# A planner's rules and one buffer: a third unit's gate inputs loaded with the first loads, and large loads held back on the queue

## The chip, the cores and the metric

The kernel runs on one core of a Trainium2 chip. The metric is the device time of one execution in microseconds (us), 591.86 as the median of three runs (590.08 to 592.78). The engines are TensorE (PE), VectorE (DVE), ScalarE (ACT), GpSimd (POOL, hardly used) and SyncE (SP), whose queue issues all DMA transfers of this kernel.

## The reference

Two stages follow each other. The first is a gated linear recurrence over time with a complex gate, for 4 batches, 8 heads, 768 steps and a head dimension of 48:

```
mag = sqrt(a_re^2 + a_im^2);  scale = min(mag, 0.999) / (mag + 1e-6)
ar, ai = a_re*scale, a_im*scale                 # per step and row d
S_re, S_im = ar*S_re - ai*S_im + k v^T,  ar*S_im + ai*S_re
y[t] = q[t] @ S_re
```

The second takes the 3072 rows of y (8 heads x 48 = 384 columns) through two matrix products with an activation between them: `h = x @ w_in` (384 x 2048), `g = 0` for h <= -1, `h` for h >= 1 and `(h+1)^2/4` between, `out = g @ w_out` (2048 x 384).

## The kernel before, in words

Time is cut into units of 256 steps: 12 units, three per batch. Two units make a block of 512 columns; there are six blocks. Three kinds of work run at once.

*Gates of a unit* (`gates(u)`). The decay and the phase of the recurrence are turned into running sums. `ai_u` holds a_re and a_im (one load of 768 KB). ACT and DVE alternate: Relu, Ln, Exp on ACT, products and clamps on DVE (L544, L547), Square and Ln on ACT, L556 and L565 on DVE; then three running sums of the decay on DVE (L575), two Exp on ACT, and the product of k and q with the decays (L594, tile `kq_u`). Then Arctan on ACT, three running sums of the phase (L604), the fraction of a turn (L620, L626), sine and cosine on ACT, and two turns on DVE: L681 makes x = kq times cosine, then kq = kq times sine. Each result is *spread* by five DMAs over the tiles `hd`, where each head has its rows together: 48, 48, 32 and twice 16 partitions. A unit thus has ten spreads, five from x and five from kq.

*Attention of a unit* (`attend(u)`). In chunks of 128 steps PE makes scores (`sc`, L834, which need all of a head's spreads), DVE masks them (`am`, L842), PE transposes keys (`tp`), ACT copies them (`kT`), PE makes state products (`dp`, L807) and DVE adds them to the state (`st`, L817, L819); PE makes the values (`yp`, L873, L881), and ACT copies them into `xr` and `ys`. After a block's last chunk six small DMAs (the hand-over, `xr<-ys`) put the rows of the split heads into their places. Then ACT and DVE split xr into a high and a low part (`xH` L967, `xL` L974).

*MoE of a block* (`moe(blk)`). For each of 16 groups of 128 hidden columns PE makes h (nine matmuls of 128x512, L997), ACT makes s from it (L1022 and, in the first block, L1032 and L1036), DVE makes g (L1041), ACT its high part (`gh`, L1055), DVE its low part (`gl`, L1059), and PE, three groups later, adds nine matmuls into the output (L1072).

*Weights* (`weights`). Sixteen pieces i0, i1, o0, i2, o1, i3, ... of 768 KB arrive as 64-bit numbers. DVE makes a float of each by two or three shifts (L401 into the one buffer `y`, L410, L419); ACT rounds it to its high part (L425). The low part is a subtraction on DVE (L430) from the fourth piece on (`LO_PE = 3`); for the first three PE forms it (`rest`, L439 and L440: float minus high part) in two halves through one PSUM bank, and ACT copies each half (L454). The raw pieces lie in buffers that later hold xH and xL: four buffers in turn for the first four pieces (`HOME = 4`), two from then on.

*Order.* All of this is recorded as operations with costs, reads, writes and due times (`Plan.op`), and `Plan.order` makes each engine's order from a list schedule. On each engine the ready operation with the earliest due time goes first. `HOLD` lets DVE and ACT stay idle for a more urgent operation that is about to be ready; SP has no such rule. Each engine's queue then runs in that order, and an operation that waits holds back all behind it. PE's idle stretches ahead of the first MoE matmul are filled with matmuls that nothing reads (L1123).

*Buffers.* Four buffers `g0` to `g3` of 768 KB hold the tiles `ai`, `x` and `kq` of the units in turn; unit 1's x, kq and V are *guests* in the places of weights that arrive late (`guest(("o", 7), ...)`). ai_2 takes g0 after ai_0, so its load waits until unit 0's last turn has read ai_0.

Of the kernel before, what the change touches and what calls it, by code (L numbers as in the profile page):

```python
# [10 lines left out]
F32 = mybir.dt.float32  # L11
# [7 lines left out]
P = 128  # L19
# [7 lines left out]
NJ = DM // P  # L27
NF = DFF // P
CH = 128
U = 256  # L30
# [24 lines left out]
LOAD, MOVE = 410.0, 240.0  # L55
TABLE = 1294
FIRST = 63000
SLACK = 1.0
LAG = 3
SPREADS = 0  # L60
SPREAD = ("SP", "ACT")
HOLD = {'DVE': (2, 0.0), 'ACT': (2, 0.0)}
WINDOW = (0.0, 0.7)
EARLY = (0.15, 0.7)
HEAD = ((15000, 8000), (8000, 2000))
HOME = 4
SPARE = 1
LEAD = 9000
WARM = 0.75
ABS_ACT = 4  # L70
LO_PE = 3
INFLATE = 1.6
SPLIT_DUE = 3000

# [38 lines left out]
class Plan:  # L113
# [43 lines left out]
    def order(self):  # L157
        ops = self.ops
        n = len(ops)
        succ = [[] for _ in range(n)]  # L160
        for i, o in enumerate(ops):
            for p in o[3]:
                succ[p].append(i)
        due = [0.0] * n
        big = 1e12
        for i in range(n - 1, -1, -1):
            eng, cost, _, _, d, dma = ops[i]
            t = big if d is None else d
            if dma:
                own = DMA_FIX + DMA_END + dma + 600  # L170
            else:
                own = cost * (INFLATE if eng in ("ACT", "DVE") else 1.0) + LAT[eng]
            for s in succ[i]:
                t = min(t, due[s] - own)
            due[i] = t
        left = [len(o[3]) for o in ops]
        ready = [0.0] * n
        end = [0.0] * n
        start = [0.0] * n
        free = {e: 0.0 for e in ("PE", "DVE", "ACT", "SP", "POOL")}  # L180
        wait = {e: [] for e in free}
        avail = {e: [] for e in free}
        queue = {}

        def enable(i):
            heapq.heappush(wait[ops[i][0]], (ready[i], i))

        for i in range(n):
            if not left[i]:
                enable(i)  # L190
        done = 0
        taken = set()
        forced = []
        while done < n:
            if forced:
                i = forced.pop()
                e = ops[i][0]
                t = max(free[e], ready[i])
            else:
                best = None  # L200
                for e in free:
                    while avail[e] and avail[e][0][1] in taken:
                        heapq.heappop(avail[e])
                    while wait[e] and wait[e][0][1] in taken:
                        heapq.heappop(wait[e])
                    if avail[e]:
                        t = free[e]
                    elif wait[e]:
                        t = max(free[e], wait[e][0][0])
                    else:  # L210
                        continue
                    if best is None or t < best[0]:
                        best = (t, e)
                t, e = best
                while wait[e] and wait[e][0][0] <= t:
                    _, i = heapq.heappop(wait[e])
                    if i not in taken:
                        heapq.heappush(avail[e], (due[i], i))
                d, i = heapq.heappop(avail[e])
                if e in HOLD:  # L220
                    late = t + ops[i][1]
                    soon = [
                        (r, j)
                        for r, j in wait[e]
                        if j not in taken
                        and r < late
                        and due[j] + HOLD[e][1] < d
                        and late - r > HOLD[e][0] * (r - t)
                    ]
                    if soon:  # L230
                        heapq.heappush(avail[e], (d, i))
                        free[e] = min(soon)[0]
                        continue
            taken.add(i)
            eng, cost, _, _, _, dma = ops[i]
            start[i] = t
            free[e] = t + cost
            if dma:
                q = queue.setdefault(eng, [0.0] * LANES)
                t = max(t, q[-LANES])  # L240
                q.append(max(t + DMA_FIX, q[-1]) + dma)
                end[i] = q[-1] + DMA_END
                start[i] = t
                free[eng] = t + cost
            else:
                end[i] = t + cost
            done += 1
            for s in succ[i]:
                left[s] -= 1
                lat = LAT[eng]  # L250
                if dma or s in self.loose:
                    lat = 0
                elif ops[s][0] == eng:
                    lat = SAME[eng]
                ready[s] = max(ready[s], end[i] + lat)
                if not left[s]:
                    enable(s)
            nxt = self.glued.get(i)
            if nxt is not None and not left[nxt]:
                forced.append(nxt)  # L260
        self.start, self.end, self.due = start, end, due
        return sorted(range(n), key=lambda i: (start[i], i))
# [44 lines left out]
def gated_scan_moe(  # L307
# [57 lines left out]

    V_, A_, PE_ = nc.vector, nc.scalar, nc.tensor

    def dma(nbytes, dst, src, r=(), w=(), due=None, rate=LOAD, eng="SP"):
        queue = {"SP": nc.sync, "ACT": nc.scalar, "POOL": nc.gpsimd}[eng]
        return pl.op(  # L370
            eng,
            DMA_ISSUE,
            lambda: queue.dma_start(dst(), src()),
            r=r,
            w=w,
            dma=nbytes / rate,
            due=due,
        )

    def table(name):  # L380
# [112 lines left out]


    heads, vt = {}, {}

    def gates(u):
        b, part = divmod(u, NPART)
        last = part == NPART - 1
        shape = [P, NJ, 2, U]  # L500
        N = NJ * U
        AI = tl(turn_of("g", 4), [P, 2, NJ, U], F32, f"ai_{u}")
        if u == 1:
            block = lambda t: t.rearrange("p (j e n) -> p j e n", j=NJ, e=2)
            X, KQ = guest(("o", 7), "x_1", block), guest(("o", 6), "kq_1", block)
# [8 lines left out]
        if u == 0:  # L514
            for e in range(2):
                dma(
                    size,
                    lambda e=e: AI.get()[:, e],
                    lambda e=e: ari[u, :, e],
                    w=[(AI, e)],  # L520
                )
        else:
            dma(2 * size, lambda: AI.get(), lambda: ari[u], w=[a, i])

        def ac(out, src, f, r, w, tab=False, **kw):
            acc_ = kw.get("accum_out")
# [63 lines left out]
        ac(X1, X0, AF.Exp, [x0], [x1], True, scale=-1.0)  # L590
        ac(X0, X0, AF.Exp, [], [x0], True)

        dma(2 * size, lambda: KQ.get(), lambda: kq[u], w=[KQ])
        ve(dve(2 * N), lambda: V_.tensor_tensor(KQ.get(), KQ.get(), X.get(), op=ALU.mult), [X], [KQ])  # L594

        yield
# [133 lines left out]
        turn(KQ, 1)  # L730
        for g in range(3):
            spread(g, 1, KQ)

# [402 lines left out]
    attend(0)  # L1138
    list(second)
    attend(1)  # L1140
    for n, (kind, i) in enumerate(todo):
        weights(n, kind, i, ("xH1", "xL1", "xH0", "xL0")[n % 4] if n < HOME else ("xH1", "xL1")[n % 2])
    for blk in range(NBLK):
        for u in BLOCKS[blk]:
            if u > 1:
                list(gates(u))
                attend(u)
        if blk == NBLK - 1:
            for k in range(NF):
# [256 lines left out]
```

## Time and profile before

| what | value |
|---|---|
| median of three runs | 591.86 us (590.08 to 592.78) |
| the profiled execution | 590.78 us, its span (first to last instruction) 589.0 us |
| busy: PE, DVE, ACT | 565.3, 448.0, 388.8 us |
| DVE busy in 0 to 20, 20 to 40, 40 to 60, 60 to 80 us | 11.17, 19.13, 14.97, 19.86 us of 20 |
| PE's granted clock, mean | 0.981 |
| first MoE matmul | 84.13 us |

PE's busy time holds the filling matmuls too, so the first 84 us are read from the waits and not from the share. In the rows, `x<-kq,ai` names what an instruction writes and reads, with buffer numbers left out; `ai<-in_ari_dram` is the load of a unit's gate inputs, `raw_i` and `raw_o` are the loads of weights.

### The profile page before, as it was taken

To read this page: it belongs to the slowest core of one execution; us is meant where nothing else is said; L and a number is where in the kernel's file an instruction comes from. 1 tells how busy PE (TensorE), PEld (TensorE's weight loads), DVE (VectorE), ACT (ScalarE), POOL (GpSimd) and SP (SyncE) were. 2 spreads that over 40 slices of the span, in tenths; PEclk is the share of its full clock that TensorE was granted. 3 is DMA by queue.
4 is the path that set the end of the run, shared out by engine and by line. 5 is a ranking of instruction groups with operands and counts; after the bars stand their busy time and mean duration, and the time that the engine had idled before them with its cause. 6 is when DMAs were issued, how large, how long until landed. Compare 5 with 4: busy or idle time off the path is not lost.

```text
span 589.0 us, 9922 instructions
## 1 busy us (share of the span) xinstructions
PE 565.3 (96%) x3920; PEld 481.1 (82%) x3920; DVE 448.0 (76%) x638; ACT 388.8 (66%) x629; POOL 1.5 (0%) x18
## 2 busy tenths in 40 slices
PE   6987989999999999999999999999999999999995
PEld 6776878888878888888888888888888888888883
DVE  4996999999988988769888788897874544555443
ACT  7756779999788675756765676656643323469962
POOL 1000000000000000000000000000000000000000
PEclk9888989999999999999999999999999999999998
DMA  8577155482561430440700530701511300077821
GB/s 348 187 202 228 47 172 200 143 303 84 160 201 37 115 128 1 117 174 20 218 24 1 168 125 19 230 13 49 154 55 55 80 1 3 19 281 260 281 84 59
DMA packets 21798, 74.26 MB, mean 126 GB/s; under 512 B 3888, under 2 KB 8496, under 8 KB 21744
## 3 DMA queue, kind: packets, MB, share of 16 engines
q1 hardware_dynamic: 21744, 73.55, 38.3%
q8 instruction: 33, 0.54, 0.4%
q14 instruction: 21, 0.17, 0.1%
HBM read 48.76 MB, written 4.72 MB: 91 GB/s over the span
## 4 chain that ended last, share of the span: by engine, by line
PE 73%; DVE 18%; ACT 4%; DMA 2%; issue 1%; DVEq 0%; ACTq 0%
PE o L1072 29%; PE h L997 29%; PE sc L834 6%; PE yp L873 2%; PE yp L881 2%; PE dp L807 2%; PE tp L778 1%; DVE am L842 1%; DVE x L681 1%; ACT ai L531 1%; DMA raw_o<-in_wl_dram 1%; DVE kq L681 1%; DVE kq L594 1%; DVE raw_i L410 1%; DVE raw_o L410 1%
## 5 line engine op out<-in xcount | busy, mean ns | idle before, releaser
L997 PE MATMUL h<-xH,wi 128*128 128x512 f32 x576 | 181.6, 396 | 1.7 <-ACT xH L967 1.2
L1072 PE MATMUL o<-gh,wo 128*128 128x512 f32 x576 | 179.5, 393 | 0.0
L997 PEld LDWEIGHTS h<-xH,wi 128*128 128x128 f32 x576 | 106.3, 189 | 23.1 <-ACT xH L967 1.4
L1072 PEld LDWEIGHTS o<-gh,wo 128*128 128x128 f32 x576 | 106.7, 188 | 21.9 <-issue 0.3
L997 PE MATMUL h<-xL,wi 128*128 128x512 f32 x288 | 113.2, 393 | 0.6 <-DVE xL L974 0.6
L1041 DVE TENSOR_TENSOR g<-h,s 128x512 f32<-128x512 f32 x96 | 65.9, 686 | 61.6 <-ACT s L1022 52.1
L1072 PE MATMUL o<-gl,wo 128*128 128x512 f32 x288 | 112.2, 390 | 0.0
L1022 ACT ACTIVATE s<-h,cst 128x512 f32<-128x512 f32 x96 | 65.9, 687 | 53.8 <-PE h L997 51.4
L1055 ACT CAST gh<-g 128x512 fp32r<-128x512 f32 x96 | 59.2, 616 | 59.1 <-DVE g L1049 58.4
L1059 DVE TENSOR_TENSOR gl<-g,gh 128x512 fp32r<-128x512 f32 x96 | 65.9, 686 | 31.0 <-ACT gh L1055 30.7
L997 PEld LDWEIGHTS h<-xL,wi 128*128 128x128 f32 x288 | 54.4, 189 | 12.7 <-DVE xL L974 1.0
L531 ACT ACTIVATE ai<-ai 128x768 f32<-128x768 f32 x52 | 43.7, 844 | 30.9 <-DVE ai L626 14.0
L1072 PEld LDWEIGHTS o<-gl,wo 128*128 128x128 f32 x288 | 54.1, 188 | 11.5
L1049 DVE SCALAR_TENSOR_TENSOR g<-s,g 128x512 f32<-128x512 f32 x80 | 55.3, 692 | 2.5
L834 PE MATMUL sc<-hd 96*128 96x128 f32 x384 | 50.4, 281 | 0.0
L834 PEld LDWEIGHTS sc<-hd 96*128 96x128 f32 x384 | 48.1, 195 | 2.6 <-DMA hd<-x 0.3
L1123 PE MATMUL idle<-mask,ident 128*128 128x128 f32 x284 | 37.5, 295 | 1.7 <-POOL mask masks.py:66 1.7
L1123 PEld LDWEIGHTS idle<-mask,ident 128*128 128x128 f32 x284 | 37.1, 211 | 2.5 <-POOL mask masks.py:66 1.7
L842 DVE TENSOR_TENSOR am<-sc,mask 128x512 f32<-128x512 f32 x48 | 32.5, 683 | 5.0 <-PE sc L834 4.7
L881 PE MATMUL yp<-am,V 128*64 128x128 f32 x384 | 35.5, 273 | 0.0
L873 PE MATMUL yp<-hd,st 96*64 96x128 f32 x320 | 32.1, 278 | 0.0
L381 ACT ACT_TABLE_LOAD x21 | 26.9, 1283 | 0.4
(87 smaller groups left out, 615.6 us busy)
## 6 DMA issues: line engine op xcount, KB each, us to landing
chk<-in_wl_dram SPq DMA_DIRECT2D x16, 768.0 KB, 5.8
kq<-in_kq_dram SPq DMA_DIRECT2D x12, 768.0 KB, 5.6
ai<-in_ari_dram SPq DMA_DIRECT2D x11, 768.0 KB, 6.6
hd<-x SPq DMA_DIRECT2D x24, 288.0 KB, 3.8
hd<-kq SPq DMA_DIRECT2D x24, 288.0 KB, 4.4
raw_i<-in_wl_dram SPq DMA_DIRECT2D x8, 768.0 KB, 5.2
raw_o<-in_wl_dram SPq DMA_DIRECT2D x8, 768.0 KB, 5.4
V<-in_v_dram SPq DMA_DIRECT2D x12, 384.0 KB, 3.3
```

The source lines that it names most:

```text
L531: lambda: A_.activation(out(), src(), f, **kw),
L834: PE_.matmul(SC.get()[:, i, :], t[:, 0, cs], t[:, 1, cs], start=True, stop=True)
L873: PE_.matmul(o, st.get().rearrange("p h e -> p (h e)")[:, lo : lo + 64], head(h)[:, 1, cs], start=True, stop=False,)
L881: PE_.matmul(o, V.get()[:, c, lo : lo + 64], ams[g].get()[:, 2 * pr + e, :], start=st is None, stop=True,)
L997: PE_.matmul(H.get(), weight["i", f // 2].get()[:, f % 2, part, sl], x.get()[:, j, :], start=j == 0 and n == 0, stop=j == NJ - 1 and n == 2,)
L1022: lambda: A_.activation(SS.get(), H.get(), AF.Relu, bias=c_half, scale=-0.5 if spare else 0.5),
L1041: lambda: V_.tensor_tensor(G.get(), H.get(), SS.get(), op=ALU.max),
L1049: lambda: V_.scalar_tensor_tensor(G.get(), SS.get(), 1.0, G.get(), op0=ALU.min, op1=ALU.mult),
L1055: pl.op("ACT", act(T), lambda: A_.copy(GH.get(), G.get()), r=[G], w=[GH])
L1059: lambda: V_.tensor_tensor(GL.get(), G.get(), GH.get().bitcast(F32), op=ALU.subtract),
L1072: PE_.matmul(PO[m].get(), weight["o", f // 2].get()[:, f % 2, part, sl], g.get(), start=f == 0 and n == 0, stop=f == NF - 1 and n == 2,)
L1123: PE_.matmul(idle["h1"], ident, mask, start=True, stop=True)
```

## The change

The changes are these:

- ai_2 becomes a guest in the place of the weight piece i5. It needs no buffer of unit 0 and can be loaded at once. The later tiles in g0 to g3 move on by one place.
- SP gets the rule of holding (`QUEUE`), and the rule counts a transfer's time as the time that the operation in hand takes. DVE and ACT hold only for operations due 2000 ns earlier.
- kq_2's and ai_3's loads may not be ordered ahead of unit 1's last spread (`moved`).
- Two buffers for the raw weights from the third piece on (`HOME` 4 to 2). The fourth piece, i2, gets its low part from PE and ACT (`LO_PE`). Unit 4's absolute value goes from DVE to ACT (`ABS_ACT`).
- The plan counts a MoE block 4% shorter (`SLACK`), and the attention of units 2 and 3 is due in the first 0.15 to 0.6 of the first block, before 0.15 to 0.7 (`EARLY`). gates(2) is recorded ahead of the weights.

```diff
-SLACK = 1.0
+SLACK = 0.96
-HOLD = {'DVE': (2, 0.0), 'ACT': (2, 0.0)}
+HOLD = {'DVE': (2, 2000.0), 'ACT': (2, 2000.0)}
+QUEUE = (1, 0.0)
-EARLY = (0.15, 0.7)
+EARLY = (0.15, 0.6)
-HOME = 4
+HOME = 2
-ABS_ACT = 4
-LO_PE = 3
+ABS_ACT = 5
+LO_PE = 4
...
                 d, i = heapq.heappop(avail[e])
-                if e in HOLD:
-                    late = t + ops[i][1]
+                hold = HOLD.get(e, QUEUE if e == "SP" else None)
+                if hold:
+                    late = t + ops[i][1] + ops[i][5]
                     soon = [
                         (r, j)
                         for r, j in wait[e]
                         if j not in taken
                         and r < late
-                        and due[j] + HOLD[e][1] < d
-                        and late - r > HOLD[e][0] * (r - t)
+                        and due[j] + hold[1] < d
+                        and late - r > hold[0] * (r - t)
                     ]
...
+    moved = []
...
-        AI = tl(turn_of("g", 4), [P, 2, NJ, U], F32, f"ai_{u}")
+        if u == 2:
+            AI = guest(("i", 5), "ai_2", lambda t: t.rearrange("p (e j n) -> p e j n", e=2, j=NJ))
+        else:
+            AI = tl(turn_of("g", 4), [P, 2, NJ, U], F32, f"ai_{u}")
...
-            dma(2 * size, lambda: AI.get(), lambda: ari[u], w=[a, i])
+            dma(2 * size, lambda: AI.get(), lambda: ari[u], w=[a, i], after=moved if u == 3 else ())
...
-        dma(2 * size, lambda: KQ.get(), lambda: kq[u], w=[KQ])
+        dma(2 * size, lambda: KQ.get(), lambda: kq[u], w=[KQ], after=moved if u == 2 else ())
...
             spread(g, 1, KQ)
+        if u == 1:
+            moved.append(len(pl.ops) - 1)
...
     attend(1)
+    list(gates(2))
     for n, (kind, i) in enumerate(todo):
         weights(n, kind, i, ("xH1", "xL1", "xH0", "xL0")[n % 4] if n < HOME else ("xH1", "xL1")[n % 2])
     for blk in range(NBLK):
         for u in BLOCKS[blk]:
+            if u > 2:
+                list(gates(u))
             if u > 1:
-                list(gates(u))
                 attend(u)
```

What this does to the orders shows at three places. The first is SP's queue from the first weights to unit 1's spreads. Names carry their numbers: `ai_2` is unit 2's load, `hd_0_1` unit 0's second head tile, the last number only names a buffer. Before, from the eighth load on:

```order
L386 DMA raw_o0_107<-in_wl_dram 128x1536
L373 DMA kq_1_109<-in_kq_dram 128x1536
L373 DMA V_0_112<-in_v_dram 128x768
L373 DMA V_1_116<-in_v_dram 128x768
L386 DMA raw_i2_120<-in_wl_dram 128x1536
L386 DMA raw_o1_191<-in_wl_dram 128x1536
L386 DMA raw_i3_256<-in_wl_dram 128x1536
L373 DMA hd_0_0_266<-x_0_114 48x1536
L373 DMA hd_0_1_268<-x_0_114 48x1536
L373 DMA hd_0_2_270<-x_0_114 32x1024
L373 DMA hd_0_2_270<-x_0_114 16x512
L373 DMA ai_2_274<-in_ari_dram 128x1536
```

and now, from the same place:

```order
L375 DMA ai_2_107<-in_ari_dram 128x1536
L375 DMA kq_1_109<-in_kq_dram 128x1536
L375 DMA V_0_112<-in_v_dram 128x768
L375 DMA V_1_116<-in_v_dram 128x768
L389 DMA raw_o0_194<-in_wl_dram 128x1536
L389 DMA raw_i2_256<-in_wl_dram 128x1536
L375 DMA hd_0_0_269<-x_0_114 48x1536
L375 DMA hd_0_1_272<-x_0_114 48x1536
L375 DMA hd_0_2_274<-x_0_114 32x1024
L375 DMA hd_0_2_274<-x_0_114 16x512
L375 DMA hd_0_0_269<-kq_0_103 48x1536
L375 DMA hd_0_1_272<-kq_0_103 48x1536
```

ai_2 stands where raw_o0 stood, raw_o0 behind V_1, and no load stands between unit 0's ten spreads; raw_o1 and raw_i3 come only after unit 1's spreads from x and from kq. Ahead of these rows raw_i0 now goes before kq_0.

The second place is ACT's queue between unit 1's last sine and unit 0's first copied keys. Before:

```order
L381 ACT_TABLE_LOAD
L425 CAST wo_0_293<-raw_o0_107 128x2x384
L531 ACTIVATE ai_2_274,fsum_89<-ai_2_274 128x768
L531 ACTIVATE x_2_342<-ai_2_274,cst_74 128x3x256
L454 CAST wo_0_293<-rest_o0_0_336 128x384
L531 ACTIVATE ai_2_274<-x_2_342 128x768
L454 CAST wo_0_293<-rest_o0_1_355 128x384
```

and now:

```order
L384 ACT_TABLE_LOAD
L538 ACTIVATE x_2_285<-ai_2_107,cst_74 128x3x256
L538 ACTIVATE ai_2_107<-x_2_285 128x768
L428 CAST wo_0_293<-raw_o0_194 128x2x384
L538 ACTIVATE ai_2_107<-ai_2_107 128x768
L457 CAST wo_0_293<-rest_o0_0_333 128x384
L538 ACTIVATE x_2_285,fsum_89<-ai_2_107 128x3x256
L538 ACTIVATE ai_2_107<-ai_2_107,cst_74 128x768
L457 CAST wo_0_293<-rest_o0_1_346 128x384
L428 CAST wi_2_367<-raw_i2_256 128x2x384
```

The Relu of ai_2 (the row with fsum) has gone from here to a place ahead of unit 1's first Exp and of the copies of i0's remainder; Ln and Exp of ai_2 stand ahead of the cast of o0.

The third place is DVE from unit 1's decay product (L594) to unit 0's masks. Before:

```order
L594 TENSOR_TENSOR kq_1_109<-kq_1_109,x_1_123 128x1536
L410 SCALAR_TENSOR_TENSOR raw_o0_107<-raw_o0_107,y_o0_279 128x768
L419 SCALAR_TENSOR_TENSOR raw_o0_107<-raw_o0_107 128x768
L681 TENSOR_TENSOR x_1_123<-kq_1_109,ai_1_98 128x1536
L681 TENSOR_TENSOR kq_1_109<-kq_1_109,ai_1_98 128x1536
L401 TENSOR_SCALAR y_i2_358<-raw_i2_120 128x768
L544 TENSOR_TENSOR ai_2_274<-ai_2_274 128x768
L547 TENSOR_SCALAR ai_2_274<-ai_2_274 128x768
L842 TENSOR_TENSOR am_0_0_0_377<-sc_0_0_0_363,mask_69 128x512
L842 TENSOR_TENSOR am_0_1_0_386<-sc_0_1_0_372,mask_69 128x512
```

and now:

```order
L601 TENSOR_TENSOR kq_1_109<-kq_1_109,x_1_120 128x1536
L422 SCALAR_TENSOR_TENSOR raw_o0_194<-raw_o0_194 128x768
L404 TENSOR_SCALAR y_i2_291<-raw_i2_256 128x768
L551 TENSOR_TENSOR ai_2_107<-ai_2_107 128x768
L554 TENSOR_SCALAR ai_2_107<-ai_2_107 128x768
L413 SCALAR_TENSOR_TENSOR raw_i2_256<-raw_i2_256,y_i2_291 128x768
L688 TENSOR_TENSOR x_1_120<-kq_1_109,ai_1_98 128x1536
L422 SCALAR_TENSOR_TENSOR raw_i2_256<-raw_i2_256 128x768
L563 SCALAR_TENSOR_TENSOR x_2_285<-ai_2_107,x_2_285 128x3x256
L851 TENSOR_TENSOR am_0_0_0_377<-sc_0_0_0_350,mask_69 128x512
L851 TENSOR_TENSOR am_0_1_0_384<-sc_0_1_0_361,mask_69 128x512
L688 TENSOR_TENSOR kq_1_109<-kq_1_109,ai_1_98 128x1536
```

The first steps of ai_2 and two shifts of i2 have moved ahead, unit 1's turn of kq has moved behind unit 0's first masks. From the second block on the orders differ only at single places.

More of the change, by code (lines that the diff above doesn't have):

```diff
@@ L366, in gated_scan_moe, with dma @@
     V_, A_, PE_ = nc.vector, nc.scalar, nc.tensor
-    def dma(nbytes, dst, src, r=(), w=(), due=None, rate=LOAD, eng="SP"):
+    def dma(nbytes, dst, src, r=(), w=(), due=None, rate=LOAD, eng="SP", after=()):
         queue = {"SP": nc.sync, "ACT": nc.scalar, "POOL": nc.gpsimd}[eng]
@@ L377, in dma @@
             due=due,
+            after=after,
         )
```

## The prediction

> **What bounds the kernel now.** The first view is that of the waits, for TensorE (PE) from 84 us on (us in all, times, longest); after 178 us it lists none.
>
> ```profile
> PE h L997 <- ACT xH L967: 1.2, 1, 1.2
> PE h L997 <- DVE xL L974: 0.6, 1, 0.6
> PE h L997 <- DVE g L1041: 0.5, 1, 0.5
> ```
>
> So from its first h matmul PE hardly waits, and that matmul's start sets the end: the kernel ends earlier by as much as it starts earlier, if VectorE (DVE), ScalarE (ACT) and the loads keep up. The second view is the timeline, where each row has the start, the length, the line, and the wait just before it in brackets:
>
> ```profile
> 73.49 1.75 DVE L681 TENSOR_TENSOR x<-kq,ai 128x1536 f32<-128x1536 f32 x1
> 75.26 2.54 SPq L373 DMA_DIRECT2D hd<-x  x4
> 78.53 4.51 SPq L373 DMA_DIRECT2D xr<-ys  x6
> 83.47 1.64 ACT L967 CAST xH<-xr 128x512 fp32r<-128x512 f32 x3
> 84.13 0.73 PE L997 MATMUL h<-xH,wi 128*128 128x512 f32 x2 [1.25 <-ACT xH L967]
> ```
>
> Unit 2's turn of x ends on DVE at 75.24; its spreads go out on SP, the hand-over (xr<-ys) stands behind them, then the casts of xH, then h at 84.13: 8.9 us after the turn. DVE's own waits between 53 and 163 us are
>
> ```profile
> DVE am L842 <- PE sc L834: 1.2, 2, 1.0
> DVE gl L1059 <- ACT gh L1055: 0.7, 1, 0.7
> DVE y_o L401 <- DMA raw_o<-in_wl_dram: 0.4, 1, 0.4
> DVE g L1041 <- ACT s L1036: 0.2, 1, 0.2
> ```
>
> 2.5 us in 110: there DVE sets PE's start and has no room. Before 53 us it has:
>
> ```profile
> 34.57 2.69 SPq L373 DMA_DIRECT2D hd<-x  x4
> 37.37 0.51 SPq L373 DMA_DIRECT2D ai<-in_ari_dram  x1
> 38.48 3.89 SPq L373 DMA_DIRECT2D hd<-kq  x5
> 45.67 0.84 ACT L531 ACTIVATE ai<-ai 128x768 f32<-128x768 f32 x1 [3.33 <-DMA ai<-in_ari_dram]
> 47.99 1.65 PE L439 MATMUL rest_o<-raw_o,ident 128*128 128x384 f32 x2 [3.16 <-ACT wo L454]
> 49.75 2.63 PE L834 MATMUL sc<-hd 96*128 96x128 f32 x16
> 48.71 0.96 DVE L544 TENSOR_TENSOR ai<-ai 128x768 f32<-128x768 f32 x1 [3.38 <-ACT ai L531]
> 51.53 0.69 DVE L842 TENSOR_TENSOR am<-sc,mask 128x512 f32<-128x512 f32 x1 [1.27 <-PE sc L834]
> 52.43 0.69 DVE L842 TENSOR_TENSOR am<-sc,mask 128x512 f32<-128x512 f32 x1 [0.20 <-PE sc L834]
> ```
>
> ai_2 is issued at 37.37, among unit 0's spreads. ACT's queue stops on it for 3.33 us, with the copy of o0's remainder behind; PE's second remainder waits 3.16 for that copy, and sc of unit 0 stands behind that. DVE stops for 3.38, 1.27 and 0.20: 4.85 us, the one real hole.
>
> **The change part by part.** *ai_2 early.* It takes the place of raw_o0 among the first loads, issued at 3.62 and landed 10.8 later; raw_o0 now waits for raw_i0's buffer. The nearest rows for that are raw_o1's load, released by the same event, and its time to landing (the second such line):
>
> ```profile
> 3.62 0.43 SPq L386 DMA_DIRECT2D raw_o<-in_wl_dram  x1
> DMA to landing us min/median/max: 10.8/10.8/10.8
> 19.77 0.33 SPq L386 DMA_DIRECT2D raw_o<-in_wl_dram  x1
> DMA to landing us min/median/max: 4.8/4.8/4.8
> 25.48 0.96 DVE L419 SCALAR_TENSOR_TENSOR raw_i<-raw_i 128x768 uint32<-128x768 uint32 x1
> 26.36 1.85 DVE L604 TENSOR_TENSOR_SCAN ai<-ai,cst 128x256 f32<-128x256 f32 x3
> 32.78 1.76 DVE L681 TENSOR_TENSOR x<-kq,ai 128x1536 f32<-128x1536 f32 x1
> ```
>
> ai_2 should thus be there at 14.4. ACT now has its Relu (0.84) ahead of the copy that frees raw_i0, so raw_o0 goes out near 20.6 and lands near 25.4. DVE comes to its first step (y_o0, now ahead of unit 0's phase scans) about 25.4, since only a short y step has moved up. No wait is the value I take, 3.5 us (ai_2's landing time, below) the other bound. The scans follow at 26.0, 0.4 earlier, but DVE now also does unit 1's fraction (L626, 0.96) ahead of unit 0's turn of x, and no sine wait is left: 26.0 + 1.77 + 0.57 + 0.97 + 0.17 + 1.96 + 0.56 + 0.96 = 33.0 instead of 32.78, and the turn of kq ends at 36.6 instead of 36.3. This is a loss of 0.3.
>
> *No large load among the spreads.* The times to landing of ai_2, of unit 0's last two spreads behind it (the later one issued at 41.5), and of unit 1's last, which has no load ahead:
>
> ```profile
> DMA to landing us min/median/max: 8.3/8.3/8.3
> L373 SPq DMA_DIRECT2D hd<-kq x2: 899/970/1042, 40.4 to 41.5; - x2
> DMA to landing us min/median/max: 7.0/7.4/7.8
> DMA to landing us min/median/max: 3.0/3.0/3.0
> ```
>
> Ten issues at 0.64 (9 spreads and a load took 34.57 to 42.37) from 34.8 end at 41.2; plus 3.0, unit 0's heads have landed at 44.2, not 48.5 (41.5 + 7.0). In the Trainium skill ("DMA: Bandwidth & Descriptors", Queues, rings and completion order) descriptors are consumed in ring order on each DMA engine, but completion is not in order per issuing engine: by that alone spreads need not wait for a load issued earlier. The 7.0 against 3.0 sides with the ring order; by the other reading the landing would stay as it was, only ACT's stop would go, and the sum below would be 0.9 in place of 4.4.
>
> *PE and DVE's new order.* Two rows more, of o0's second shift and of unit 1's turn of kq:
>
> ```profile
> 40.44 0.96 DVE L419 SCALAR_TENSOR_TENSOR raw_o<-raw_o 128x768 uint32<-128x768 uint32 x1
> 43.10 1.76 DVE L681 TENSOR_TENSOR kq<-kq,ai 128x1536 f32<-128x1536 f32 x1
> ```
>
> o0's shifts now end on DVE at 36.6 + 0.87 + 1.67 + 0.90 = 40.0 (41.4 before). From there to sc took 8.35 us, 3.33 of it ACT's stop: 40.0 + 5.0 = 45.0, later than the landing. The masks were ready to start 1.78 and 2.68 us after sc's start, so the second is done by 48.4. Unit 1's turn of kq now stands behind these masks: done at 50.1, where before it was done at 44.86 with the masks behind it. Ahead of them lie 9.8 us of work from 36.6, so DVE waits from 46.4 for about 0.6 + 0.3. Bounds: 49.3 if no mask has to be waited for (46.4 + 1.2 + 1.7), 52 if the heads land 2.8 us later than worked out. Then come, up to the end of unit 2's turn of x, at the step from one DVE start to the next, 0.07 to 0.1 under the means of these rows:
>
> ```profile
> L842 DVE TENSOR_TENSOR am<-sc,mask 128x512 f32<-128x512 f32 x15 | 10.0, 678 | 1.2 <-PE sc L834 1.2
> L410 DVE SCALAR_TENSOR_TENSOR raw_o<-raw_o,y_o 128x768 uint32<-128x768 uint32 x6 | 5.7, 957 | 0.0
> L681 DVE TENSOR_TENSOR x<-kq,ai 128x1536 f32<-128x1536 f32 x3 | 5.2, 1750 | 0.0
> L575 DVE TENSOR_TENSOR_SCAN x<-x,state,cst 128x256 f32<-128x256 f32 x6 | 4.4, 739 | 0.0
> ```
>
> six masks 3.6, five of the 128x768 kind (L565, L410, L419, L626, wo1's L430) 4.5, six scans 4.0, two 1536-wide (L594, L681) 3.4, three states, two y steps, the round and the copy 2.9: 18.4. Check on the old trace: 53.03 + 18.4 + i2's two shifts and low part, x_2's L556 (3.6) = 75.0; measured 75.24. The low part of i2 (0.87) is off DVE: PE and ACT do it between sc and yp (by o0's row above 1.65 us on PE at most, twice, and two ACT copies), while DVE has the turn of kq, L565 and three scans, 4.5 us. Without that cover it costs up to 1 us. New waits in the stretch (st behind dp, phase scans behind ACT's Arctan, masks behind sc) were nearly nothing before; I take 2.0, bounds 0.5 and 4. End of the turn: 50.1 + 18.4 + 2.0 = 70.5, against 75.24: **4.7 earlier**. The 8.9 us after it stay: five spread issues still stand ahead of the hand-over.
>
> *Other moves.* raw_i0 ahead of kq_0: it lands one place later, some 2 us (seven loads in 14.4), and is used only after both units' decay scans; without that cover the 2 us would count. raw_o1 and raw_i3 leave only after unit 1's spreads (47.8, 53.5); with 4.8 to land they are there before DVE wants them (55 and 66). Unit 1's kq spreads, out by 53.4, land by 57; their sc follows unit 0's last dp near 59. Only 2 us of cover, and 3 of cost if it fails as behind ai_2. Two weight buffers in place of four had been the rule from the fifth piece on. Downstream, DVE enters the first MoE block owing one shift of o2 more (0.87) and unit 4's Abs less (0.56), so PE's wait of 0.5 at 163 grows to 0.8. Sum: 4.7 - 0.3 = 4.4.
>
> **The rivals.** *A, the clock (584.7).* PE idles ahead of h, and then
>
> ```profile
> 81.90:85.30 3.40, 1.71 (x11) 1.08 (x10) 3.37 (x6) 3.37 (x7) 0.00 (x0) 1.00 0.47 116
> 85.30:88.70 3.40, 3.28 (x8) 2.61 (x9) 3.37 (x6) 1.45 (x2) 0.00 (x0) 0.50 0.57 171
> ```
>
> the granted clock is 0.50 for 3.4 us (1.7 lost). With h at 79.4 these boundaries fall elsewhere, and the slow stretch may be missed: 1.7 more gain. The Trainium skill ("TensorE: Matmul & The Clock Gate", What's actually happening) has a free-running 3.4 us window; the trace's stretch is as long. Against: idle time ahead of h remains, and the window may hit again. *B, given back (589).* PE starts 4.4 earlier, but DVE or ACT find new waits of 2 to 3 us between 90 and 160 us, or unit 1's spreads land 3 late: gain 1.5 to 2. For it: the 2.5 us of slack in 110. Against: that stretch's rows hardly change in content. *C, the wait changes its place (590).* Masks, remainder of i2 and the late turn of kq in one line take back the 4.85: waits of 6 instead of 2.0 in the stretch, gain 0.4; or the heads still land at 48.5 and sc waits 3.5 us for them, gain 0.9. For it: three queues now meet in one line there. Against: DVE's work in the stretch is the same 18.4 us and no longer shares it with ai_2's first steps. *D, slower (594).* If ai_2 lands at 23 instead of 14.4 (as late against its place as the 8.3 us above), ACT stops on its Relu, the copy behind it frees raw_i0 8.4 late, raw_o0 goes out at 28.2 and lands at 33, and DVE stands at y_o0 for 7.6 with unit 0's scans behind: 590.8 - 4.4 + 7.6 = 594.0. It decides from a landing of raw_o0 at 30 (no gain left). Against: the same bytes stood there before.
>
> **How the numbers follow.** The profiled execution took 590.78 us, 1.78 beyond its span and 1.1 below the median of 591.86; 590.78 - 4.4 = **586.4**. Forecast (585 to 588) 0.50, A 0.15, B 0.17, C 0.09, D 0.09. The bounds (waits 0.5 to 4, turn 49.3 to 52, with A's clock) give 582.5 to 590.5, which holds 0.8. About 0.5% (3 us) is what can be told from no change: faster 0.70 (forecast, A, a little of B), same 0.21, slower 0.09.
>
> **What would show it.** Right: no ACT wait on ai's load near 45; sc of unit 0 at 44 to 46; unit 2's turn of x ending near 70.5; h at 79 to 80; no PE wait above 1 us after it. Wrong: DVE waiting over 1 us at y_o near 25 (D); waits at masks, st or phase scans between 50 and 70 adding to over 4 (C); PE waits on g, gl or xL after 90 (B); h at 79.4 and still the old end.

## The result, and the profile after

The changed kernel takes 586.3 us (median of 6 runs, 584.22 to 587.72) against 591.61 for the kernel before beside it: ratio 0.9907, 95% interval 0.9881 to 0.9933. The profiled execution took 584.84 us with a span of 583.1, 5.9 under the span before. The forecast was 586.4. The number is right; the reason given for it is only partly so, as the experiments show. The ratios in this document are the ones on record and not always the quotient of the two medians. One execution of the change without SP's rule, 595.56 us at a granted clock of 0.977, was in a slow state and is left out of its median and ratio.

First the stretch up to the first h, in the timeline of the changed kernel (start, length, engine, line, operation; in brackets the wait just before). It answers to the second and fourth view of the prediction:

```profile
25.06 0.56 DVE L404 TENSOR_SCALAR y_o<-raw_o 128x768 uint32<-128x768 uint32 x1
34.60 2.70 SPq L375 DMA_DIRECT2D hd<-x  x4
44.02 1.95 PE L843 MATMUL sc<-hd 96*128 96x128 f32 x16
45.90 1.28 DVE L851 TENSOR_TENSOR am<-sc,mask 128x512 f32<-128x512 f32 x2
47.10 1.75 DVE L688 TENSOR_TENSOR kq<-kq,ai 128x1536 f32<-128x1536 f32 x1
53.72 0.56 DVE L404 TENSOR_SCALAR y_o<-raw_o 128x768 uint32<-128x768 uint32 x1 [0.82 <-DMA raw_o<-in_wl_dram]
66.72 1.74 DVE L688 TENSOR_TENSOR x<-kq,ai 128x1536 f32<-128x1536 f32 x1
71.87 4.59 SPq L375 DMA_DIRECT2D xr<-ys  x6
76.89 1.66 ACT L976 CAST xH<-xr 128x512 fp32r<-128x512 f32 x3 [0.34 <-DMA xr<-ys]
77.56 0.73 PE L1006 MATMUL h<-xH,wi 128*128 128x512 f32 x2 [1.90 <-ACT xH L976]
```

DVE's hole of 4.85 us near 50 is gone: no wait stands at the first y_o, none at the masks. Unit 2's turn of x ends at 68.46 (75.24 before), the first h starts at 77.56 (84.13 before).

Second, where PE stops from the first h on. This answers to the first view of the prediction; the rows are those of PE's timeline that carry a wait on DVE:

```profile
122.11 0.74 PE L1006 MATMUL h<-xH,wi 128*128 128x512 f32 x2 [1.46 <-DVE g L1050]
153.33 0.73 PE L1006 MATMUL h<-xH,wi 128*128 128x512 f32 x2 [0.30 <-DVE g L1050]
157.58 0.72 PE L1006 MATMUL h<-xH,wi 128*128 128x512 f32 x2 [0.56 <-DVE g L1050]
```

2.3 us, all behind DVE's g in the first MoE block; before it was 0.5, in one stop:

```profile
163.50 0.72 PE L997 MATMUL h<-xH,wi 128*128 128x512 f32 x2 [0.46 <-DVE g L1041]
```

So h starts 6.6 us earlier, but PE then runs into DVE.

Third, the largest of DVE's waits between its first instruction and the last low part of a weight (L430 before, L433 after, tile wo), and DVE's busy time in that stretch. Before:

```profile
DVE ai L544 <- ACT ai L531: 5.0, 2, 3.4
DVE am L842 <- PE sc L834: 2.5, 3, 1.3
```

```profile
7.00:167.40 160.40, 145.72 (x1177) 125.97 (x1176) 149.68 (x200) 129.43 (x198) 0.00 (x0) 0.95 0.57 186
```

And of the changed kernel:

```profile
DVE y_o L404 <- DMA raw_o<-in_wl_dram: 1.9, 2, 1.1
DVE kq L601 <- ACT s L1045: 1.7, 1, 1.7
DVE y_i L404 <- DMA raw_i<-in_wl_dram: 0.6, 1, 0.6
```

```profile
7.60:161.35 153.75, 139.93 (x1148) 119.73 (x1147) 147.10 (x199) 129.25 (x201) 0.00 (x0) 0.98 0.59 192
```

In the windows the third number after the stretch's length is DVE's busy time: it was idle for 160.40 - 149.68 = 10.7 us before and is for 153.75 - 147.10 = 6.65 now. DVE reaches that last low part 6.05 us earlier: it has 4.1 us less idle time and 2.6 less work, and begins 0.6 later. Where it ends, and where the program's last matmul (fp) starts, before:

```profile
166.42 0.95 DVE L430 TENSOR_TENSOR wo<-raw_o,wo 128x768 fp32r<-128x768 f32 x1
581.49 0.19 PE L1174 MATMUL fp<-ok,cst 128*1 128x4 f32 x2
```

and after:

```profile
160.37 0.96 DVE L433 TENSOR_TENSOR wo<-raw_o,wo 128x768 fp32r<-128x768 f32 x1
575.58 0.19 PE L1185 MATMUL fp<-ok,cst 128*1 128x4 f32 x2
```

From the one to the other 415.1 us pass before and 415.2 after. From the first h to fp it is 497.4 and 498.0. Two executions cannot say which of the two sets the end; the experiments were chosen for that.

### The profile page after: what moved, and what is told of

Read it like the earlier page. It is cut to its first block, busy times and chain, and to the rows that moved or that the text cites. A ratio compares the mean times of both kernels' runs of the same rounds, so it can differ in the third digit from the quotient of the medians.

```text
span 583.1 us, 9888 instructions
## 1 busy us (share of the span) xinstructions
PE 560.2 (96%) x3904; PEld 475.6 (82%) x3904; DVE 445.3 (76%) x636; ACT 388.2 (67%) x632; POOL 1.5 (0%) x18
## 4 chain that ended last, share of the span: by engine, by line
PE 72%; DVE 14%; ACT 5%; DMA 5%; issue 2%; SPq 1%; ACTq 0%; DVEq 0%
PE o L1081 29%; PE h L1006 29%; PE sc L843 5%; DMA raw_o<-in_wl_dram 3%; PE yp L882 2%; PE yp L890 2%; PE dp L816 2%; ACT ai L538 2%; DVE ai L611 2%; PE tp L787 1%; ACT x L538 1%; DVE gl L1068 1%; DMA raw_i<-in_wl_dram 1%; SPq L375 1%; DVE g L1050 1%
## 5 line engine op out<-in xcount | busy, mean ns | idle before, releaser
L1132 PE MATMUL idle<-mask,ident 128*128 128x128 f32 x262 | 34.5, 294 | 1.7 <-POOL mask masks.py:66 1.7
L1132 PEld LDWEIGHTS idle<-mask,ident 128*128 128x128 f32 x262 | 33.9, 210 | 2.4 <-POOL mask masks.py:66 1.7
```

Of the source, the lines that this page charges most:

```text
L1132: PE_.matmul(idle["h1"], ident, mask, start=True, stop=True)
```

## The experiments

Three theories stood at the start. **T**: ACT's stop on ai_2, and what PE and its clock lose behind it, carry the gain. **H**: SP's new rule carries it, by keeping large loads from among the spreads. **K**: the new constants carry it, by another order of the steps.

### One part alone, one part taken out

The guest alone, on the kernel before:

```
+        if u == 2:
+            AI = guest(("i", 5), "ai_2", ...)
...
+    list(gates(2))          # ahead of the weights, as in the change
```

> The kernel before with one thing of the change: ai_2 as a guest in i5's place (and gates(2) recorded ahead of the weights). Theory T (the gain is ACT's stop on ai_2's load, with PE's idle and half-clock time behind it): no ACT wait on ai's load after 20 us, no load among unit 0's spreads, gain 3.5 to 6 us, 585.5 to 588 against 591.6. Rival H (the gain is the rule of holding on SP): at most 1.5 us gained, 590 or more. Rival K (the gain is the new constants): no gain, 591 to 592.

SP's rule alone, on the kernel before:

```
+QUEUE = (1, 0.0)
+                hold = HOLD.get(e, QUEUE if e == "SP" else None)
+                    late = t + ops[i][1] + ops[i][5]
```

> The kernel before with the rule of holding on SP alone (with the transfer's time counted). ai_2 still waits for unit 0's buffer and is still ordered behind unit 0's first four spreads. T: the stop on ai_2 stays, 590.5 to 592.5. H: gain 3 us or more, 588.5 or less. K: 591 to 592.

The change without the guest, and the change without SP's rule:

```
-        if u == 2:
-            AI = guest(("i", 5), "ai_2", ...)
+        AI = tl(turn_of("g", 4), [P, 2, NJ, U], F32, f"ai_{u}")
```

> The changed kernel with ai_2 back in its buffer g0 behind ai_0; hold, two raw buffers and all constants as changed. T: ACT stops 3 us or more on ai's load near 45 us again, most of the gain is lost: 590 to 593. H and K: the gain stays, 586 to 588.

```
-                hold = HOLD.get(e, QUEUE if e == "SP" else None)
+                hold = HOLD.get(e)
```

> The changed kernel without holding on SP: raw_o1 goes ahead of unit 1's spreads, raw_i3 between those of x and those of kq. T: ai_2 is early all the same, a loss of 0 to 2 us: 586 to 588.5. H: the gain is gone, 590 or more. K: 586 to 587.

Measured, with the kernel before at 591.6 on the same chip: guest alone 595.07 (ratio 1.0059, 1.0042 to 1.0077), rule alone 594.88 (1.0038, 1.0008 to 1.0068), change without the guest 596.82 (1.0107, 1.0070 to 1.0144), change without the rule 588.6 (0.9944, 0.9923 to 0.9964). Each part alone makes the kernel slower by about half a per cent, and each part taken out costs: 11.8 us for the guest, 2.2 for the rule (differences of the ratios to 0.9907, times 591.5; for the rule the two intervals overlap, so its price is uncertain by some 2 us). As single causes all three theories fail: H forecast 588.5 or less for the rule alone, K forecast that the change without the guest keeps the gain. T fails at the first run, although there h does start earlier, at 80.27 instead of 84.13: DVE meets a new wait in block 0, at i5's load, and its waits for sc, most of them ahead of h, are 3.3 us in place of 2.5:

```profile
DVE y_i L401 <- DMA raw_i<-in_wl_dram: 3.4, 1, 3.4
DVE am L845 <- PE sc L837: 3.3, 3, 1.9
```

That h comes 3.9 us earlier and the end 1 us later (in the profiled executions) is what a start that sets the end does not allow. Two new theories came from it. **S**, the prediction's own: PE is the bound from its first h on. **D**: DVE's queue, up to the last low part of block 0, is the bound, and PE only waits for it.

### Clock alone, PE alone, DVE alone

More filler matmuls in the kernel before, meant to keep PE's clock up; the other instructions keep their order:

```
-WARM = 0.75
+WARM = 0.95
```

> The kernel before with more filler matmuls in TensorE's planned gaps (the filler factor 0.95 in place of 0.75), no other instruction moved. It is the clock alone. S (TensorE sets the end from its first h matmul): the half-clock stretches go, the last of which cost 1.7 us at 85.3 and the earlier ones about 0.7 each ahead of unit 0's sc: 588.5 to 590 us against 591.6. D (VectorE's queue up to the last decoded weight of block 0, 167.4 us, sets the end): TensorE only arrives earlier at its stop near 162, and of VectorE's waits only those for sc shrink: 590.3 to 592 us.

591.41 us, ratio 1.0002 (0.9987 to 1.0017). An earlier stretch, the windows of 3.4 us ahead of and behind the first h, and the three rows that count:

```profile
47.30:57.55 10.25, 9.07 (x39) 8.46 (x40) 5.82 (x8) 6.87 (x12) 0.00 (x0) 0.50 0.86 275
81.90:85.30 3.40, 3.40 (x33) 3.40 (x32) 3.33 (x6) 2.73 (x5) 0.00 (x0) 1.00 0.38 101
85.30:88.70 3.40, 3.10 (x21) 2.52 (x20) 3.40 (x5) 3.40 (x6) 0.00 (x0) 1.00 0.56 149
```

```profile
86.69 0.71 PE L997 MATMUL h<-xH,wi 128*128 128x512 f32 x2
167.06 0.95 DVE L430 TENSOR_TENSOR wo<-raw_o,wo 128x768 fp32r<-128x768 f32 x1
582.13 0.19 PE L1174 MATMUL fp<-ok,cst 128*1 128x4 f32 x2
```

The granted clock is 1.00 behind the first h, where it was 0.50, and the median is the same: S forecast 588.5 to 590, and its range is missed. But this run is not the clock alone. PE stood at 0.50 for 10.25 us at 47.3, where the kernel before had 6.8 us of half clock between 41 and 51, and h started 2.6 us later than before. The last low part came 0.64 later, and the end moved by 0.64. S's own account comes near that too (h 2.6 later, 1.7 of clock back, 0.4 less of stops: 0.5), so this trace does not tell S from D. Nor was every execution alike: the four with a granted clock of 0.993 or 0.994 took 588.9 to 590.9 us, the seven with 0.986 to 0.990 took 591.4 to 593.6; whether the clock makes that difference is not shown.

Nine matmuls of h, group 12 of block 0, done twice over in the changed kernel (2.06 us in the trace):

```
+                    for _ in range(AGAIN if (blk, f, j) == (0, 12, 0) else 0):
+                        PE_.matmul(H.get(), ..., start=True, stop=True)
```

> The changed kernel with nine h matmuls of block 0's group 12 (near 148 us) done twice over: 9 x 0.23 = 2.05 us more work on TensorE, same output, no order changed. S: every microsecond that TensorE loses after its start is lost at the end: 586.3 + 2.0 = 588.3 us. D: TensorE stops behind VectorE's g at 152 to 157 anyway (1.2 us in all in the changed kernel's trace), so most of it is hidden: 586.3 to 587.2 us, and the stop at 156.6 gets smaller.

And two microseconds of DVE work, the first decode step of i7 done five times:

```
-            lambda: V_.tensor_scalar(Y.get(), top(), 3, 0x3FFFFFFF, ...),
+            lambda: [V_.tensor_scalar(Y.get(), top(), 3, 0x3FFFFFFF, ...)
+                     for _ in range(TWICE.get((kind, i), 1))],
```

> The changed kernel with the first decode step of the weight i7 (near 137.4 us, 0.5 us) done five times instead of once: 2.0 us more work on VectorE, same output, no order changed. S: VectorE is off the path there and has some slack: 586.3 to 587.0 us. D: the last decoded weight of block 0 comes 2.0 us later and the end with it: 588.3 us or a little more, if the longer stop of TensorE lowers its clock (up to 1.7 us: 590).

PE with more work: 585.02 us, ratio 0.9898 (0.9883 to 0.9913), no loss against the change's 0.9907. DVE with more work: 587.71, ratio 0.9941 (0.9927 to 0.9956), which is 0.0034 x 591.5 = 2.0 us over the change; five steps take 2.92 us in the trace where one took 0.54, so 2.4 were added. The interval of the change reaches up to 0.9933, so the 2.0 is uncertain by nearly as much. The firmer comparison is that of these two runs, made on one chip: about the same work costs 0.0043 x 591.2 = 2.5 us more on DVE than on PE, and their intervals lie apart. The rows of the second, in which PE waits behind the added steps:

```profile
136.54 2.92 DVE L406 TENSOR_SCALAR y_i<-raw_i 128x768 uint32<-128x768 uint32 x5
141.63 0.51 PE L886 MATMUL yp<-hd,st 96*64 96x128 f32 x4 [2.52 <-DVE am L855]
161.86 0.95 DVE L437 TENSOR_TENSOR wo<-raw_o,wo 128x768 fp32r<-128x768 f32 x1
577.13 0.19 PE L1189 MATMUL fp<-ok,cst 128*1 128x4 f32 x2
```

The times lie nearer to D's forecasts (586.3 to 587.2, and 588.3) than to S's (588.3, and up to 587.0), and S, by which the added matmuls had to cost 2.0, falls. Not all of D shows in the traces: the profiled execution of the run with more PE work is the slowest of its five, 4.6 us over their median, and PE has no stop behind DVE there after 126.4. So in that one PE itself sets the pace from there on, and the added work is not seen to be hidden. Over all fourteen profiled executions of this study (their own times, which in single cases lie up to 5 us off the medians), in us from the span's start; "idle" is DVE's idle time between its first instruction and the last low part:

| kernel | time | first h | last low part | fp | fp - h | fp - low part | idle |
|---|---|---|---|---|---|---|---|
| before | 590.8 | 84.13 | 166.42 | 581.49 | 497.4 | 415.1 | 10.7 |
| changed | 584.8 | 77.56 | 160.37 | 575.58 | 498.0 | 415.2 | 6.6 |
| guest alone | 592.9 | 80.27 | 168.08 | 582.55 | 502.3 | 414.5 | 12.5 |
| rule alone | 595.3 | 84.54 | 170.91 | 585.98 | 501.4 | 415.1 | 14.1 |
| change, no guest | 595.7 | 81.31 | 171.93 | 586.37 | 505.1 | 414.4 | 17.4 |
| change, no rule | 589.5 | 78.98 | 163.63 | 580.27 | 501.3 | 416.6 | 8.8 |
| before, more fillers | 591.4 | 86.69 | 167.06 | 582.13 | 495.4 | 415.1 | 11.3 |
| change, PE +2 | 589.7 | 79.79 | 165.20 | 580.43 | 500.6 | 415.2 | 11.1 |
| change, DVE +2 | 586.5 | 77.14 | 161.86 | 577.13 | 500.0 | 415.3 | 5.8 |
| two constants back | 591.6 | 77.60 | 167.74 | 582.32 | 504.7 | 414.6 | 10.6 |
| change, i5 late | 592.0 | 78.84 | 167.57 | 582.76 | 503.9 | 415.2 | 13.4 |
| two constants back, i5 first | 591.2 | 77.78 | 167.18 | 582.01 | 504.2 | 414.8 | 10.0 |
| change, o4 first | 585.7 | 79.15 | 160.81 | 576.43 | 497.3 | 415.6 | 6.9 |
| change, due times back | 587.8 | 80.05 | 163.86 | 578.45 | 498.4 | 414.6 | 9.1 |

The time from the first h to the end varies by 9.6 us, that from the last low part by 1.2 in thirteen of the fourteen. The fourteenth, without SP's rule, has a half-clock stretch of PE at 160.7 to 164.1, right ahead of the low part; that this is its 1.5 us more was not tried. The last low part is a mark on DVE's queue, not shown to be what PE waits for: PE's last stop in the changed kernel is behind g, at 157.58. Nor does the constant by itself say which engine leads, since it holds in the run with more PE work too; it says that the two engines are in step there. What leads is told by the runs in which one engine's work or waits were changed.

### The constants

```
-ABS_ACT = 5
+ABS_ACT = 4
-LO_PE = 4
+LO_PE = 3
```

> The changed kernel with two of its constants set back: the Abs of the fifth angle tile on VectorE again (0.56 us) and the low part of the weight i2 too (0.87 us). The planner also puts kq_0 ahead of raw_i0 again and raw_o0 behind. S: the stretch up to h has one step of 0.87 more, h at 78.4: 587.2 us. D: 1.4 us more VectorE work ahead of the last decoded weight, and whatever waits the new order of the first weights brings: 588 to 592 us. If the constants carry no part of the gain: 586.3 us.

591.25 us, ratio 1.0001 (0.9978 to 1.0023): with these two set back, nothing of the gain is left in the median, although h starts at 77.60, as in the change. That is S's plainest miss. (The twelve executions fall in two groups: seven, at a granted clock of 0.984 to 0.989, took 588.1 to 591.6 us; five, at 0.978 to 0.983, took 593.0 to 594.6. What parts them was not looked for.) The planner's order is another one too: the load of i2 goes out at 49.93 instead of 29.49. DVE has three steps more ahead of the last low part (201 instead of 198), and waits, most at i5's first step:

```profile
120.03 0.56 DVE L404 TENSOR_SCALAR y_i<-raw_i 128x768 uint32<-128x768 uint32 x1 [4.05 <-DMA raw_i<-in_wl_dram]
```

The load it waits for was issued at 110.1 behind three of unit 3's spreads of x and took 9.9 us to land, where in the kernel before the same load, ahead of them, took 4.3. It is the prediction's case of ai_2 again, one unit later. With the guest alone it is the same load (7.2 us, the wait of 3.4 above).

### A large load among spreads, by hand

The order that the planner gives was changed at one place each time; the first lets i5's load in the changed kernel stand behind three spreads, the second puts it ahead in the kernel with the two constants back, the third puts o4's load of the changed kernel ahead of the spreads of kq:

```
         order = self.order()
+        for i, j in self.behind(order):
+            order.remove(i)
+            order.insert(order.index(j) + 1, i)
```

> The changed kernel with one issue on SP moved: the load of the weight i5 (issued at 103.1 us, ahead of unit 3's spreads of x) now stands behind the third of them. L (a large load among spreads lands late, and VectorE, whose queue sets the end of block 0, waits for it): the load goes out near 106.6 and takes 7 to 9 us to land as in the runs with guest alone and with the constants set back, so VectorE waits 3.5 to 5.5 us at i5's first step instead of 0.6, and the end comes 3 to 5 us later: 589 to 591 us. Not L (those waits were a by-product of the other order, and something behind takes them up): 586 to 587 us.

> The kernel with the two constants set back, and the load of i5 (there issued at 110.1 us between unit 3's spreads of x, landed 119.0 to 120.0, VectorE waiting 4.05 us) put ahead of all of them; nothing else moved. L: the load leaves when its buffer is free, near 109.6, and lands 4.3 later at 113.9 plus what other transfers take; the wait of 4.05 falls to 0.5 or less and the end comes 2.5 to 3.5 us earlier: 588 to 589 us against 591.3. If only the constants' VectorE work (1.4 us and the steps moved with it) made the difference: 591 us as before.

> The changed kernel with the load of o4 (issued at 111.0 us behind three of unit 3's spreads of kq, landed 117.5, VectorE waiting 1.1 us for it) put ahead of these spreads, where its buffer is free at 108.8; nothing else moved. L: it lands near 114, the wait of 1.1 us goes, and the end comes about 1 us earlier: 585.2 us, a little less if the later spreads of kq make unit 3's sc late. Not L: 586.3 us.

Late in the change: 589.89 us, ratio 0.9970 (0.9948 to 0.9991), 3.7 us lost to one issue moved by three places. The load's row on SP's queue, and DVE's step behind it, in an execution of 592.04 us:

```profile
107.70 0.53 SPq L392 DMA_DIRECT2D raw_i<-in_wl_dram  x1
116.70 0.56 DVE L409 TENSOR_SCALAR y_i<-raw_i 128x768 uint32<-128x768 uint32 x1 [7.90 <-DMA raw_i<-in_wl_dram]
```

The wait of 7.9 is more than the 3.5 to 5.5 forecast. It is 7.3 us longer than in the change's trace, and the last low part comes 7.2 later. Most of that is not the landing: the load goes out 4.6 us later (107.70 instead of 103.10), since the spreads ahead of it stand on SP's queue until DVE's turn of x is done, and it then takes 9.0 us to land instead of 6.2.

First with the constants back: 591.2 us, ratio 1.0000 (0.9986 to 1.0015); the forecast gain of 3 us did not come. The wait of 4.05 is gone, and the next load takes it over: o4's, behind the spreads of kq, landed 7.1 after its issue:

```profile
123.76 0.56 DVE L409 TENSOR_SCALAR y_o<-raw_o 128x768 uint32<-128x768 uint32 x1 [2.76 <-DMA raw_o<-in_wl_dram]
```

DVE's last low part comes 0.6 earlier and no more, so the lost gain there is not this one wait. With the constants back DVE reaches that low part 7.4 us later than in the change, 4.0 of it idle and the rest in steps; how much of the steps is the two that the constants name (0.87 and 0.56) and how much the order was not separated.

o4 first in the change: 585.66 us, ratio 0.9893 (0.9870 to 0.9917). Its wait of 1.1 at o4's first step is gone from the trace, but i5's grew from 0.6 to 1.5 in this execution. It is 0.8 us under the change, with intervals that overlap: neither shown nor excluded.

### The due times

```
-SLACK = 0.96
+SLACK = 1.0
-EARLY = (0.15, 0.6)
+EARLY = (0.15, 0.7)
```

> The changed kernel with the planner's two due-time constants set back (SLACK 1.0, EARLY 0.15 to 0.7): up to the first h the order is the same, behind it TensorE's groups and VectorE's steps are interleaved otherwise. If the stops of TensorE in block 0 of the changed kernel (2.8 us) come from these constants: 584 to 585 us. By VectorE's queue (the same 150 us of work ahead of the last decoded weight but for one g more, 0.6 us): 586 to 587.5 us.

585.72 us, ratio 0.9893 (0.9870 to 0.9917), not to be told from the change, and between the two ranges that were forecast. That these two constants make the stops in block 0 is not shown: the profiled execution still has 1.9 us of PE's stops behind DVE, against 2.3, and h starts 2.5 us later in it. The two kernels at 585.7 beat the kernel before; that they beat the change is not shown.

## Why the prediction was right, and where it was not

**"That matmul's start sets the end."** This premise failed. The row it was read from, PE's wait of 0.5 on g near 163, was the sign of the other thing: PE had just caught up with DVE there, and in every other kernel measured PE stops behind DVE somewhere in the first block too. The sentence beside it, that DVE "has no room" in these 110 us, was the right reading, and should have carried the sum. The forecast came out because the gain was worked out along DVE's steps up to unit 2's turn of x, and DVE's time is what counts. That it came within 0.1 us is luck: it set out from the profiled 590.78, where the median beside the change was 591.61, and the gain was forecast as 4.4 where the medians give 5.3 and the profiled executions 5.9.

**The hole of 4.85 us.** Right. DVE has no wait from 22 to 53 us. raw_o0 landed at 25.03 (forecast 25.4) and y_o0 started at 25.06; the heads of unit 0 landed at 44.13 (44.2). Unit 0's last spreads, issued at 39.3 to 40.9, took

```profile
DMA to landing us min/median/max: 3.3/3.7/4.4
```

instead of 7.0 to 7.8. So the spreads landed sooner once no load stood ahead of them. That agrees with the ring order which the Trainium skill describes ("DMA: Bandwidth & Descriptors", Queues, rings and completion order). That completion need not be in order, which the section says too, shows in none of the eight executions looked at for it: all 243 transfers of SP's queue landed in the order of their issue.

**Loss of 0.3 ahead of it.** None: unit 0's turn of x ended at 34.58 (34.8), as before.

**Unit 1's turn of kq at 50.1.** It ended at 48.85, under the lower bound of 49.3, since sc came at 44.02 (45.0) and both masks without a wait at 45.90. PE had full clock there; in the profile before it had half clock at 41 to 44. That this brought sc forward was not tried.

**2.0 us of new waits in the stretch.** 1.2: 0.82 for o1's load and 0.38 for kq_2's. o1 was said to be there before DVE wants it; it landed 5.6 us after its issue (4.8 taken) and was wanted 0.8 earlier.

**4.7 earlier at the end of the turn of x, then 8.9 to h.** 6.8 and 9.1; h 6.57 earlier instead of 4.7.

**Downstream -0.3.** This is the term that was mis-sized most: 2.3 us of stops on g instead of 0.8, one of them (1.46) over the 1 us that was named as a sign. It is rival B, "given back", with 1.8 us more stops than before instead of 2 to 3; it goes with the earlier h, since DVE's end of block 0 moves by 6.05 and PE's start by 6.57, and in the first block PE no longer loses its half-clock stretch.

**Rival A, the clock.** It happened (granted clock 1.00 behind the first h). The times do not part it from the forecast: the median is 586.3, but the profiled execution, at 584.84, lies at A's 584.7. The rows speak against its price. In the trace before PE still stops 0.46 us behind g at 163.50, after the half-clock stretch, and DVE in between waits 0.9 us for ACT, so most of the time won in that stretch would only have lengthened this stop: A's price of 1.7 us is too high, for the same reason as the premise. This is argued from those waits; the run with more fillers, which was to show it, lost clock elsewhere.

**Rival C** (waits of 6 in the stretch) and **D** (raw_o0 late) did not happen. But D's mechanism, DVE standing behind a late load, costs DVE 2.3 to 7.9 us at one load in eight of the profiled executions (rule alone, guest alone, change without the guest, change without the rule, PE with more work, constants back, the same with i5 first, i5 late).

**What the sum left out.** The two constants that take i2's low part to PE and an Abs to ACT were costed as cover and as parts of the stretch. If DVE's queue leads, they are gain in full. Setting them back takes all of the gain in the median, more than their own 1.4 us, but it also gives another order, and the two were not separated. By the lengths in the trace, DVE's work ahead of the last low part fell by 1.7: one low part 0.95, one Abs 0.56, one g that now stands behind 0.72, less one more update of st 0.54. The remaining 0.9 of the 2.6 lies in how close the records stand, and was not traced.

**What stays open.** Why the parts do not add up is shown only in examples: each change makes the planner order everything anew, and moving one large load among the spreads, with nothing else, cost 3.7 us in one run but won nothing clear of the noise in two others. That this is all of the differences between guest alone, rule alone and the change is not shown.

## What to carry to other kernels

When an engine "hardly waits" from some point on, look at what its few remaining waits name: if they all name one other engine, and that engine has no room, the two may run in step, and it may be the other's queue that sets the end; two microseconds of harmless extra work on each, in turn, tell which. Follow then the bound engine's last instruction that the rest depends on, not the first one of the busiest. And where a planner orders the queues, expect that a part of a change cannot be judged alone: look in each new order for the large loads among small urgent ones first.

## What was not expected of the hardware

A half-clock stretch of PE need not cost anything where PE still has to stop for DVE later, as at 163.50 in the kernel before, but it can cost where DVE waits for PE. Three of the kernels that share the change's order up to h had h at 79.2 to 80.1 instead of 77.6. All three had a load of o1 that landed later, half clock from 56 us on, and a wait of DVE for dp. The windows of one of them (o4 first), and DVE's wait:

```profile
52.40:55.80 3.40, 1.83 (x20) 1.61 (x20) 1.96 (x4) 3.34 (x6) 0.00 (x0) 1.00 1.01 283
55.80:59.20 3.40, 3.40 (x42) 3.40 (x39) 2.82 (x4) 1.78 (x3) 0.00 (x0) 0.51 1.01 346
```

```profile
60.13 0.55 DVE L838 TENSOR_TENSOR st<-st,dp 96x384 f32<-96x384 f32 x1 [1.48 <-PE dp L826]
```

o1's load landed 0.6 us later than in the change, DVE's mask behind it too, PE was busy for only 1.83 of 3.4 us, its clock was 0.51 for the next 3.4, and DVE waited 1.48 for dp. In the change's own execution the same stretch had 2.44 us busy and kept its clock:

```profile
52.90:56.30 3.40, 2.44 (x35) 2.23 (x35) 2.55 (x4) 3.37 (x5) 0.00 (x0) 1.00 1.04 239
```

So 0.6 us at a load was followed by 1.5 at DVE, here as in the other two. The Trainium skill ("TensorE: Matmul & The Clock Gate", Why this matters for your kernels) advises no idle gaps of PE above about 3 us; here the clock fell behind a window whose one gap was 1.57 us. The busy time alone does not decide it, though. Another of the three (due times back) kept its clock behind a window with less of it:

```profile
76.68:80.09 3.41, 1.54 (x15) 1.35 (x13) 3.20 (x5) 2.95 (x5) 0.00 (x0) 1.00 0.23 53
80.09:83.50 3.41, 3.41 (x18) 2.67 (x19) 3.38 (x6) 1.72 (x4) 0.00 (x0) 1.00 0.67 172
```

What decides it was not found.
